# Attention with a token-routed feed-forward: the MoE of each batch as two streams, set into the attention loop by a table

## The chip, the cores and the metric

One core of a Trainium2 chip runs the kernel. The metric is device time in microseconds, taken around the whole program; the kernel before needs 296.96 us (median of three runs, 294.28 to 300.0). One more execution was recorded by the hardware profiler and took 294.19 us, of which 291.8 us lie between its first and its last instruction.

## The reference: what is computed

Two parts, one after the other. The attention (8 batches, 12 heads, 448 tokens, head size 64) has a squared ReLU in place of the softmax; its result `x` is the input of a mixture-of-depths layer (hidden size 768, inner size 1024), which passes only the 128 tokens with the highest gate score of each batch through two matrices and adds the result, weighted with a sigmoid of the score, to those tokens.

```python
scores = scale * q @ k.T                      # per batch and head, 448 x 448
x = (np.maximum(scores, 0.0) ** 2 / S) @ v    # heads side by side: 448 x 768
score = x @ w_gate                            # 448 values of a batch
top_idx = np.argpartition(-score, 128)[:128]
h = np.maximum(x[top_idx] @ w1, 0.0)
out = x.copy()
out[top_idx] += sigmoid(score[top_idx])[:, None] * (h @ w2)
```

## The kernel before: how the work is tiled and ordered

Inputs are loaded as bf16 by DMAs that POOL issues (`load`, lines 79 to 100), a batch at a time into one of three buffers; `load(b + 2)` is issued at the start of batch `b`. The loop runs over 48 iterations `t`, each one pair of heads (six to a batch). Its parts:

- `transposes(t)` (L160, L166): 16 matmuls against the identity put q and k of the pair, transposed, into one PSUM tile, which VectorE copies to `qkt` (L171).
- `scores(t, c)` (L181, L185): for the key chunks 0 to 2 two matmuls, one for each head, each on 64 rows of the TensorE array (contraction 64); chunk 3 is one matmul on all 128 rows (the two heads' last 64 keys each, in a zero-padded form). `s_ps` has two buffers.
- `relu_square(t, c)`: ScalarE applies the ReLU (L193), VectorE squares (L194).
- `attend(t, c)` (L205): two matmuls, each on 64 columns of the array, accumulate chunk `c` into `o_ps`; after the last chunk ScalarE scales it into `xT` (L211).

So TensorE works in three array modes: row halves (scores of chunks 0 to 2), column halves (transposes, attend) and the full array (chunk 3 and all of the MoE but a few small steps).

The MoE of a batch, `moe(b)` (lines 217 to 331), is one generator: gate scores (L222, then `bc`, L225), `x` transposed back in four chunks (`x_chunk`, L231, copied by VectorE, L234), the scores as columns (L240 and a chain of five small VectorE steps, L243 to L249), the rank of every token by comparing it with all others (`rank_chunk`, L256, four times), a one-hot matrix (`hot`, L272), the list of chosen tokens (`sel`, L279), the gathering matmuls (`xe`, L296), the two matrices (`h`, L307; `ye`, L320) and an indirect DMA that adds the result to the output (L327), behind a plain DMA of all of `x` (L268). All its PSUM tiles rotate through one pool of two buffers, `m_ps`. `advance` runs the generator from two places of each iteration, as far as the costs written into its `yield`s allow; the MoE of a batch is spread so over the six iterations of the next batch, and the last one follows the loop.

The order is written out by hand; each engine runs its instructions in that order, so an instruction that waits holds up all that follow it on its engine.

```python
for t in range(NT + 1):
    scores(t, 0); scores(t, 1); relu_square(t, 0); relu_square(t, 1)
    attend(t - 1, 2); attend(t - 1, 3)
    transposes(t + 1)
    advance(share)
    scores(t, 2); scores(t, 3); relu_square(t, 2); relu_square(t, 3)
    attend(t, 0); attend(t, 1)
    advance(share)
```

Of the kernel before, what the change touches and what calls it, by code (L numbers as in the profile page):

```python
# [20 lines left out]
def kernel(  # L21
# [27 lines left out]
    qt_pool = ctx.enter_context(tc.tile_pool(name="qt", bufs=3))  # L49
# [10 lines left out]
    m_ps_pool = ctx.enter_context(tc.tile_pool(name="m_ps", bufs=2, space=PSUM))  # L60
# [156 lines left out]
    def moe(b):  # L217
        xTb = xT.pop(b)
        x_sb = x_pool.tile([P, NC, HD], BF16, name="x_sb")
        sc_ps = m_ps_pool.tile([128, S], FP32, name="sc_ps", tag="m")  # L220
        for m in range(NM):
            nc.tensor.matmul(out=sc_ps, lhsT=wg_rep[:, m, :], rhs=xTb[:, m, :],  # L222
                             start=(m == 0), stop=(m == NM - 1))
        bc = small.tile([128, S], FP32, name="bc")
        nc.scalar.copy(out=bc, in_=sc_ps)  # L225
        yield 1.1

        def x_chunk(c):
            x_ps = m_ps_pool.tile([P, HD], BF16, name="x_ps", tag="m")
# [6 lines left out]
        x_chunk(0)  # L236
        yield 0.35
        col_ps = m_ps_pool.tile([P, NC], FP32, name="col_ps", tag="m")
        for c in range(NC):
            nc.tensor.matmul(out=col_ps[:, c:c + 1], lhsT=bc[0:1, c * P:(c + 1) * P],  # L240
                             rhs=one_f, is_transpose=True, start=(c == 0), stop=(c == NC - 1))
        cols = small.tile([P, NC], FP32, name="cols")
        nc.vector.tensor_copy(out=cols, in_=col_ps)  # L243
        tk = tok[b % 2]
        rem = small.tile([P, NC], FP32, name="rem")
        nc.vector.tensor_copy(out=tk[:, :, 2], in_=cols)
        nc.vector.tensor_tensor(out=rem, in0=cols, in1=tk[:, :, 2], op=ALU.subtract)
        nc.vector.tensor_copy(out=tk[:, :, 3], in_=rem)
        nc.vector.tensor_tensor(out=tk[:, :, 4], in0=rem, in1=tk[:, :, 3], op=ALU.subtract)  # L249
        yield 0.3  # L250

        rank = small.tile([P, NC], FP32, name="rank")
        trash = small.tile([P, S], BF16, name="trash")

        def rank_chunk(c):
# [19 lines left out]
        yield 0.6

        sel_ps = m_ps_pool.tile([CAP, 5], FP32, name="sel_ps", tag="m")
        for c in range(NC):
            nc.tensor.matmul(out=sel_ps, lhsT=hot[:, c, :], rhs=tk[:, c, :],  # L279
                             start=(c == 0), stop=(c == NC - 1))  # L280
        sel = small.tile([CAP, 5], FP32, name="sel")
        nc.vector.tensor_copy(out=sel, in_=sel_ps)
        idx = small.tile([CAP, 1], INT32, name="idx")
        nc.vector.tensor_tensor(out=idx, in0=sel[:, 0:1], in1=sel[:, 1:2], op=ALU.add)
        g = small.tile([CAP, 1], FP32, name="g")
        nc.vector.scalar_tensor_tensor(out=g, in0=sel[:, 4:5], scalar=sel[:, 3:4],
                                       in1=sel[:, 2:3], op0=ALU.add, op1=ALU.add)
        yield 0.2

        xeT = moe_pool.tile([128, NM, CAP], BF16, name="xeT")  # L290
        for half in range(2):
            ps = m_ps_pool.tile([128, 3, CAP], FP32, name="xe_ps", tag="m")
            for mm in range(3):
                m = half * 3 + mm
                for c in range(NC):
                    nc.tensor.matmul(out=ps[:, mm, :], lhsT=x_sb[:, c, m * 128:(m + 1) * 128],  # L296
                                     rhs=hot[:, c, :], start=(c == 0), stop=(c == NC - 1))
            nc.scalar.copy(out=xeT[:, half * 3:half * 3 + 3, :], in_=ps)  # L298
            yield 0.67

        hT = moe_pool.tile([128, NF, CAP], BF16, name="hT")
        for half in range(2):
            ps = m_ps_pool.tile([128, 4, CAP], FP32, name="h_ps", tag="m")
            for ff in range(4):
                f = half * 4 + ff
                for m in range(NM):
                    nc.tensor.matmul(out=ps[:, ff, :], lhsT=w1_sb[:, m, f * 128:(f + 1) * 128],  # L307
                                     rhs=xeT[:, m, :], start=(m == 0), stop=(m == NM - 1))
                if ff == 1:
                    yield 0.67  # L310
            nc.scalar.activation(out=hT[:, half * 4:half * 4 + 4, :], in_=ps, func=AF.Relu)
            yield 0.67

        nc.scalar.activation(out=g, in_=g, func=AF.Sigmoid)
        gye = moe_pool.tile([CAP, HD], FP32, name="gye")
        for half in range(2):
            cols_d = slice(half * 384, half * 384 + 384)
            ps = m_ps_pool.tile([CAP, 384], FP32, name="ye_ps", tag="m")
            for f in range(NF):
                nc.tensor.matmul(out=ps, lhsT=hT[:, f, :], rhs=w2_sb[:, f, cols_d],  # L320
                                 start=(f == 0), stop=(f == NF - 1))
                if f == 3:
                    yield 0.66
            nc.scalar.activation(out=gye[:, cols_d], in_=ps, func=AF.Copy, scale=g[:, 0:1])  # L324
            if half == 0:
                yield 0.66
        nc.gpsimd.indirect_dma_start(  # L327
            out=out.rearrange("b s d -> (b s) d"),
            out_offset=bass.IndirectOffsetOnAxis(ap=idx[:, :1], axis=0),
            in_=gye, in_offset=None, element_offset=b * S * HD, compute_op=ALU.add)  # L330
        yield 0.66


    MOE_US = 9.7
    active = []
    credit = [0.0]

    def advance(us):
        if not active:
            credit[0] = 0.0  # L340
            return
        credit[0] += us
        while active and credit[0] > 0.0:
            try:
                credit[0] -= next(active[0])
            except StopIteration:
                active.pop(0)

    tc_manual = tc.manual_schedule()
    with tc_manual:  # L350
        transposes(0)
        share = MOE_US / (2 * NHP) * 1.05
        for t in range(NT + 1):
            b, hp = divmod(t, NHP)
            if t < NT:
                scores(t, 0)
                scores(t, 1)
                relu_square(t, 0)
                relu_square(t, 1)
            if t > 0:  # L360
                attend(t - 1, 2)
                attend(t - 1, 3)
                if t % NHP == 0:
                    active.append(moe(t // NHP - 1))
            if t < NT:
                if hp == 0 and b + 2 < B:
                    load(b + 2, 0, H)
                if t + 1 < NT:
                    transposes(t + 1)
                advance(share)  # L370
                scores(t, 2)
                scores(t, 3)
                relu_square(t, 2)
                relu_square(t, 3)
                attend(t, 0)
                attend(t, 1)
                advance(share)
        while active:
            advance(10.0)
# [35 lines left out]
```

## Time and profile before

| | |
|---|---|
| median of three runs | 296.96 us (294.28 to 300.0) |
| profiled execution | 294.19 us, span 291.8 us |
| PE (TensorE matmul) busy | 231.8 us, 79% of the span |
| ACT (ScalarE) busy | 196.8 us, 67% |
| DVE (VectorE) busy | 184.4 us, 63% |
| POOL (GpSimd) busy | 88.8 us, 30% |
| mean granted TensorE clock | 0.918 of full speed |
| data moved | 34.20 MB |

Busy time is the union of the intervals in which an engine has an instruction running. A matmul's end is modelled and matmuls overlap, so what a matmul costs is read from start to start, not from its duration. The shares are means over stages with different limits: a head that waits for loads, six batches of like work, and a tail after the last head pair.

### The profile page before, as it was taken

The page shows a single profiled execution, that of the slowest core. Times are in us where ns is not written, and L with a number is a line of the kernel's source. Part 1 is how long each engine was busy: PE and PEld are TensorE (multiplying, and loading weights), DVE is VectorE, ACT ScalarE, POOL GpSimd, SP SyncE. Part 2 cuts the span into 40 slices and gives each one's busy share as a digit, 9 for nine tenths or more (in the row PEclk, how much of TensorE's full clock was granted, in tenths as well). Part 3 has the DMA queues.
Part 4 walks back from the last instruction along what each step waited for, and adds up shares of the span by engine and source line. Part 5 has one row for each costly group of instructions (what it writes and reads, how often), then busy time and mean ns, then how long its engine had stood idle before and what let it go on. Part 6 is the DMA issues. An engine that isn't in the chain of part 4 may idle for free.

```text
span 291.8 us, 6198 instructions
## 1 busy us (share of the span) xinstructions
PE 231.8 (79%) x2496; PEld 132.2 (45%) x2496; DVE 184.4 (63%) x426; ACT 196.8 (67%) x306; POOL 88.8 (30%) x128
## 2 busy tenths in 40 slices
PE   1598924799959997899978998699869995997570
PEld 1144413355436644465445644464436542644550
DVE  4268742955696658835696658956796669755400
ACT  1389940589846987458875996689759995794130
POOL 8989206771181027100541018100200020002010
PEclk9999995699998999579986999999999999999595
DMA  3999999999599709950399009950322030403504
GB/s 42 104 144 125 211 208 173 170 196 194 198 127 180 223 0 142 201 189 2 40 173 286 31 0 138 202 191 2 55 80 113 0 56 1 191 0 49 195 0 54
DMA packets 41723, 34.20 MB, mean 117 GB/s; under 512 B 14944, under 2 KB 39008, under 8 KB 40800
## 3 DMA queue, kind: packets, MB, share of 16 engines
q0 software_dynamic: 41696, 33.83, 69.6%
q8 instruction: 19, 0.31, 0.4%
q14 instruction: 8, 0.07, 0.1%
HBM read 39.32 MB, written 14.16 MB: 183 GB/s over the span
## 4 chain that ended last, share of the span: by engine, by line
PE 46%; DVE 19%; DMA 10%; ACT 9%; POOL 8%; issue 5%; POOLq 1%; ACTq 0%
PE o_ps L205 10%; PE s_ps L181 9%; PE h_ps L307 7%; ACT r_sb L193 7%; DMA k_sb<-in_k_dram 7%; PE ye_ps L320 7%; DVE trash L256 5%; DVE a_sb L194 4%; PE xe_ps L296 4%; DVE x_sb L234 4%; PE s_ps L185 3%; DMA q_sb<-in_q_dram 2%; PE t_ps L166 2%; DMA out_dram<-x_sb 2%; POOL k_sb L89 2%
## 5 line engine op out<-in xcount | busy, mean ns | idle before, releaser
L193 ACT ACTIVATE r_sb<-s_ps 128x896 bf16<-128x896 f32 x192 | 148.2, 829 | 48.4 <-PE s_ps L181 47.6
L194 DVE TENSOR_TENSOR a_sb<-r_sb 128x896 bf16<-128x896 bf16 x192 | 103.4, 564 | 69.2 <-ACT r_sb L193 68.5
L205 PE MATMUL o_ps<-a_sb,v_sb 128*64 128x448 bf16 x384 | 59.5, 384 | 3.0 <-DVE a_sb L194 2.6
L327 POOL DMA_INDIRECT out_dram<-gye,idx x8 | 13.1, 1638 | 127.1 <-ACT gye L324 117.9
L181 PE MATMUL s_ps<-qkt 64*128 64x448 bf16 x288 | 49.2, 376 | 2.7 <-ACT r_sb L193 1.3
L171 DVE COPY qkt<-t_ps 128x960 bf16<-128x960 bf16 x48 | 31.2, 651 | 14.1 <-PE t_ps L166 14.1
L205 PEld LDWEIGHTS <-v_sb 128*64 128x64 bf16 x384 | 19.2, 110 | 33.0 <-issue 27.5
L160 PE MATMUL t_ps<-ident,q_sb 112*64 112x112 bf16 x384 | 19.6, 225 | 15.5 <-DMA q_sb<-in_q_dram 10.1
L307 PE MATMUL h_ps<-xeT,w_sb 128*128 128x128 bf16 x384 | 28.0, 227 | 1.3 <-ACT xeT L298 1.3
L160 PEld LDWEIGHTS <-q_sb 112*64 112x64 bf16 x384 | 17.8, 118 | 21.4 <-DMA q_sb<-in_q_dram 15.8
L92 POOL DMA_DIRECT2D v_sb<-in_v_dram x22 | 17.5, 796 | 31.8 <-DMA q_sb<-in_q_dram 12.5
L231 PE MATMUL x_ps<-ident,xT_sb 128*112 128x128 bf16 x192 | 16.7, 231 | 12.6 <-DVE x_sb L234 10.6
L211 ACT ACTIVATE xT_sb<-o_ps 128x448 bf16<-128x448 f32 x48 | 26.6, 554 | 0.1
L307 PEld LDWEIGHTS <-w_sb 128*128 128x128 bf16 x384 | 23.3, 102 | 5.3 <-issue 4.0
L181 PEld LDWEIGHTS <-qkt 64*128 64x128 bf16 x288 | 12.6, 94 | 27.9 <-issue 19.5
L320 PE MATMUL ye_ps<-w_sb,hT 128*128 128x384 bf16 x128 | 25.0, 328 | 0.0
L298 ACT CAST xeT<-xe_ps 128x384 bf16<-128x384 f32 x16 | 7.6, 478 | 25.0 <-PE xe_ps L296 24.3
L166 PE MATMUL t_ps<-ident,k_sb 128*64 128x128 bf16 x384 | 21.9, 232 | 2.7 <-DMA k_sb<-in_k_dram 2.6
L89 POOL DMA_DIRECT2D v_sb<-in_v_dram x22 | 20.1, 921 | 8.6 <-DMA w_sb<-in_moe_w_dram 7.2
L231 PEld LDWEIGHTS <-xT_sb 128*112 128x112 bf16 x192 | 13.8, 137 | 17.6 <-issue 17.1
L256 DVE SCALAR_TENSOR_TENSOR trash<-bc,cols,tie 112x448 bf16<-112x448 f32 x32 | 21.7, 677 | 0.0
L89 POOL DMA_DIRECT2D k_sb<-in_k_dram x22 | 20.9, 954 | 0.0
(54 smaller groups left out, 217.6 us busy)
## 6 DMA issues: line engine op xcount, KB each, us to landing
out_dram<-x_sb POOLq DMA_DIRECT2D x8, 1344.0 KB, 8.8
q_sb<-in_q_dram POOLq DMA_DIRECT2D x6, 672.0 KB, 9.8
w_sb<-in_moe_w_dram POOLq DMA_DIRECT2D x2, 1536.0 KB, 14.4
k_sb<-in_k_dram POOLq DMA_DIRECT2D x12, 192.0 KB, 10.0
v_sb<-in_v_dram POOLq DMA_DIRECT2D x12, 192.0 KB, 6.9
k_sb<-in_k_dram POOLq DMA_DIRECT2D x12, 144.0 KB, 9.9
v_sb<-in_v_dram POOLq DMA_DIRECT2D x12, 144.0 KB, 10.8
q_sb<-in_q_dram POOLq DMA_DIRECT2D x2, 224.0 KB, 4.3
```

The costliest lines, as they stand in the source:

```text
L89: nc.gpsimd.dma_start(out=t[0:64, hs, 0:lo, :], in_=src[b, hs, 0:64 * lo].rearrange("h (p c) d -> p h c d", c=lo))
L160: nc.tensor.matmul(out=ps[64 * hh:64 * hh + 64, c * P:(c + 1) * P], lhsT=qs[:, h0 + hh, c, :], rhs=ident[:P, :P], is_transpose=True, start ...
L166: nc.tensor.matmul(out=ps[64 * hh:64 * hh + 64, S + c * 128:S + (c + 1) * 128], lhsT=ks[:, h0 + hh, c, :], rhs=ident, is_transpose=True, s ...
L171: nc.vector.tensor_copy(out=sb, in_=ps)
L181: nc.tensor.matmul(out=ps[:, hh, :S], lhsT=sb[rows, S + c * 128:S + (c + 1) * 128], rhs=sb[rows, :S], start=True, stop=True)
L193: nc.scalar.activation(out=r[:, :n], in_=ps[:, :n, :S], func=AF.Relu)
L194: nc.vector.tensor_tensor(out=a[:, :n], in0=r[:, :n], in1=r[:, :n], op=ALU.mult)
L205: nc.tensor.matmul(out=o_ps[t][rows, :], lhsT=vs[:, 2 * hp + hh, c, :], rhs=a[:, hh if c < 3 else 0, :], start=(c == 0), stop=(c == 3), sk ...
L231: nc.tensor.matmul(out=x_ps[:, m * 128:(m + 1) * 128], lhsT=xTb[:, m, c * P:(c + 1) * P], rhs=ident, is_transpose=True, start=(m == 0), st ...
L256: nc.vector.scalar_tensor_tensor(out=trash, in0=bc[:P, :], scalar=cols[:, c:c + 1], in1=tie[:, c, :], op0=ALU.subtract, op1=ALU.is_ge, acc ...
L307: nc.tensor.matmul(out=ps[:, ff, :], lhsT=w1_sb[:, m, f * 128:(f + 1) * 128], rhs=xeT[:, m, :], start=(m == 0), stop=(m == NM - 1))
L320: nc.tensor.matmul(out=ps, lhsT=hT[:, f, :], rhs=w2_sb[:, f, cols_d], start=(f == 0), stop=(f == NF - 1))
```

## The change

The attention loop is reordered: the transposes run two iterations ahead (with four `qkt` buffers), all of `attend(t - 1)` stands together behind the first two scores of `t`, in the chunk order 0, 1, 3, 2, and the second half of an iteration computes chunk 3 before chunk 2. The MoE is split in two sets of steps. `moe_rank(b)` (gate to gathering) runs during batch `b + 1`, `moe_ffn(b)` (the two matrices) during batch `b + 2`; two tables say which steps stand in which of the twelve half iterations. The pool `m_ps` of two buffers becomes two pools of one buffer each: `ma_ps` (gate, columns, `x`, `sel`, first half of `xe`) and `mb_ps` (second half of `xe`, `h`, `ye`). What each step computes is as before.

```diff
...
-    qt_pool = ctx.enter_context(tc.tile_pool(name="qt", bufs=3))
+    qt_pool = ctx.enter_context(tc.tile_pool(name="qt", bufs=4))
...
-    m_ps_pool = ctx.enter_context(tc.tile_pool(name="m_ps", bufs=2, space=PSUM))
+    ma_ps_pool = ctx.enter_context(tc.tile_pool(name="ma_ps", bufs=1, space=PSUM))
+    mb_ps_pool = ctx.enter_context(tc.tile_pool(name="mb_ps", bufs=1, space=PSUM))
...
-                             stop=(c == 3), skip_group_check=True)
-        if c == 3:
+                             stop=(c == 2), skip_group_check=True)
+        if c == 2:
...
-    def moe(b):
+    def moe_rank(b):
...
+        def gate(m0, m1):
+            if m0 == 0:
+                ps["sc"] = ma_ps_pool.tile([128, S], FP32, name="sc_ps", tag="m")
+            for m in range(m0, m1):
+                nc.tensor.matmul(out=ps["sc"], lhsT=wg_rep[:, m, :], rhs=xTb[:, m, :],
+                                 start=(m == 0), stop=(m == NM - 1))
+            if m1 == NM:
+                nc.scalar.copy(out=bc, in_=ps["sc"])
...
+        def gather(half):
+            xe = (ma_ps_pool, mb_ps_pool)[half].tile([128, 3, CAP], FP32, name="xe_ps", tag="m")
...
+    def moe_ffn(b, idx, g, xeT):
...
+        def hidden(f):
+            if f % 4 == 0:
+                ps["h"] = mb_ps_pool.tile([128, 4, CAP], FP32, name="h_ps", tag="m")
+            for m in range(NM):
+                nc.tensor.matmul(out=ps["h"][:, f % 4, :],
+                                 lhsT=w1_sb[:, m, f * 128:(f + 1) * 128],
+                                 rhs=xeT[:, m, :], start=(m == 0), stop=(m == NM - 1))
+            if f % 4 == 3:
+                nc.scalar.activation(out=hT[:, f - 3:f + 1, :], in_=ps["h"], func=AF.Relu)
...
+        def project(half, f0, f1):
...
+    RANK = {
+        1: [("gate", 0, 6)], 2: [("col",)], 3: [("x", 0)], 4: [("x", 1), ("rank", 0)],
+        5: [("rank", 1)], 6: [("x", 2)], 7: [("rank", 2)], 8: [("x", 3), ("rank", 3)],
+        9: [("hot",)], 10: [("sel",)], 11: [("xe", 0), ("xe", 1)],
+    }
+    FFN = {
+        0: [("h", 0)], 1: [("h", 1)], 3: [("h", 2), ("h", 3)],
+        5: [("h", 4), ("h", 5), ("h", 6), ("h", 7)], 7: [("y", 0, 0, 8)], 9: [("y", 1, 0, 8)],
+    }
...
+    def moe(b, hs):
+
+        if b >= 1:
+            if hs == 1:
+                rank_steps[b - 1], handed[b - 1] = moe_rank(b - 1)
+            if hs >= 1:
+                place(RANK, rank_steps[b - 1], hs)
+        if b >= 2:
+            if hs == 0:
+                ffn_steps[b - 2] = moe_ffn(b - 2, *handed.pop(b - 2))
+            place(FFN, ffn_steps[b - 2], hs)
+
+    with tc.manual_schedule():
         transposes(0)
...
+        transposes(1)
+        for t in range(NT):
             b, hp = divmod(t, NHP)
...
+            scores(t, 0)
+            scores(t, 1)
+            relu_square(t, 0)
+            relu_square(t, 1)
             if t > 0:
...
+                for c in (0, 1, 3, 2):
+                    attend(t - 1, c)
+            if hp == 0 and b + 2 < B:
+                load(b + 2, 0, H)
+            if t + 2 < NT:
+                transposes(t + 2)
+            moe(b, 2 * hp)
+            scores(t, 3)
+            relu_square(t, 3)
+            scores(t, 2)
+            relu_square(t, 2)
+            moe(b, 2 * hp + 1)
+        for c in (0, 1, 3, 2):
+            attend(NT - 1, c)
+        for hs in range(12):
+            moe(B, hs)
+        ffn_steps[B - 1] = moe_ffn(B - 1, *handed.pop(B - 1))
+        for hs in range(12):
+            place(FFN, ffn_steps[B - 1], hs)
```

## Rows read from the trace of the kernel before

**Rows 1.** Windows: stretch, length, busy us of each engine, TensorE clock, DMA share, GB/s.

```profile
27.07:30.50 3.43, 2.95 (x34) 1.45 (x31) 2.74 (x5) 3.41 (x6) 3.43 (x7) 1.00 1.03 150
...
74.97:106.90 31.93, 27.95 (x315) 15.94 (x314) 22.93 (x52) 24.05 (x38) 8.64 (x11) 0.95 0.77 140
106.90:140.64 33.74, 30.49 (x313) 17.56 (x313) 22.45 (x52) 24.24 (x38) 8.54 (x11) 0.85 0.68 116
...
172.69:203.36 30.67, 26.84 (x315) 15.28 (x314) 22.32 (x52) 24.22 (x38) 8.53 (x11) 1.00 0.75 127
...
264.96:291.80 26.84, 12.69 (x128) 10.07 (x126) 6.36 (x21) 4.56 (x10) 3.76 (x3) 0.74 0.35 81
```

**Rows 2.** Waits of PE, 75 to 265 us: sum, times, longest (us).

```profile
PE x_ps L231 <- DVE x_sb L234: 7.7, 6, 3.2
PE sel_ps L279 <- DVE hot L272: 7.5, 5, 2.4
```

**Rows 3.** Timeline of PE, one iteration and a little more: start, us, instructions.

```profile
223.68 1.51 PE L307 MATMUL h_ps<-xeT,w_sb 128*128 128x128 bf16 x24
225.13 0.55 PE L181 MATMUL s_ps<-qkt 64*128 64x448 bf16 x4
225.61 0.57 PE L205 MATMUL o_ps<-a_sb,v_sb 128*64 128x448 bf16 x4
226.01 0.37 PE L160 MATMUL t_ps<-ident,q_sb 112*64 112x112 bf16 x8
...
226.53 0.84 PE L307 MATMUL h_ps<-xeT,w_sb 128*128 128x128 bf16 x12
227.31 0.36 PE L181 MATMUL s_ps<-qkt 64*128 64x448 bf16 x2
227.61 0.36 PE L185 MATMUL s_ps<-qkt 128*128 128x448 bf16 x1
227.90 0.57 PE L205 MATMUL o_ps<-a_sb,v_sb 128*64 128x448 bf16 x4
228.40 0.82 PE L320 MATMUL ye_ps<-w_sb,hT 128*128 128x384 bf16 x4
229.16 0.69 PE L181 MATMUL s_ps<-qkt 64*128 64x448 bf16 x4
```

**Rows 4.** Timeline of DVE, 241 to 245 us.

```profile
241.33 0.65 DVE L171 COPY qkt<-t_ps 128x960 bf16<-128x960 bf16 x1
241.90 0.15 DVE L243 COPY cols<-col_ps 112x4 f32<-112x4 f32 x1
...
242.78 0.68 DVE L256 SCALAR_TENSOR_TENSOR trash<-bc,cols,tie 112x448 bf16<-112x448 f32 x1
...
243.39 0.55 DVE L234 COPY x_sb<-x_ps 112x768 bf16<-112x768 bf16 x1
243.86 0.92 DVE L194 TENSOR_TENSOR a_sb<-r_sb 128x896 bf16<-128x896 bf16 x2
```

**Rows 5.** Timeline of ACT, first two ReLUs of that iteration (225.13 in Rows 3).

```profile
225.53 1.73 ACT L193 ACTIVATE r_sb<-s_ps 128x896 bf16<-128x896 f32 x2 [0.37 <-PE s_ps L181]
```

**Rows 6.** Timeline of PE: transposes of t = 8 and of t = 12.

```profile
48.92 0.61 PE L166 MATMUL t_ps<-ident,k_sb 128*64 128x128 bf16 x7 [0.93 <-DMA k_sb<-in_k_dram]
...
71.82 0.39 PE L160 MATMUL t_ps<-ident,q_sb 112*64 112x112 bf16 x8
```

**Rows 7.** Timeline of POOL: the last k load of batch 2 is issued.

```profile
52.88 0.69 POOL L92 DMA_DIRECT2D k_sb<-in_k_dram  x1
```

**Rows 8.** The page's DMA issues: KB each, median us to landing.

```profile
k_sb<-in_k_dram POOLq DMA_DIRECT2D x12, 192.0 KB, 10.0
```

**Rows 9.** Timeline of the tail, PE and ACT.

```profile
272.89 0.27 PE L279 MATMUL sel_ps<-tok,hot 112*128 112x5 bf16 x4 [2.98 <-DVE hot L272]
...
273.02 2.72 PE L296 MATMUL xe_ps<-hot,x_sb 112*128 112x128 bf16 x24
...
282.57 0.58 ACT L324 ACTIVATE gye<-ye_ps,g 128x384 f32<-128x384 f32 x1 [0.67 <-PE ye_ps L320]
```

More of the change, by code (lines that the diff above doesn't have):

```diff
@@ L212, in attend, with columns @@
                                  scale=o_scale)
-    def moe(b):
+    def moe_rank(b):
         xTb = xT.pop(b)
         x_sb = x_pool.tile([P, NC, HD], BF16, name="x_sb")
[L220 to L223, printed above, removed]
         bc = small.tile([128, S], FP32, name="bc")
-        nc.scalar.copy(out=bc, in_=sc_ps)
-        yield 1.1
+        cols = small.tile([P, NC], FP32, name="cols")
+        rem = small.tile([P, NC], FP32, name="rem")
+        rank = small.tile([P, NC], FP32, name="rank")
+        trash = small.tile([P, S], BF16, name="trash")
+        hot = small.tile([P, NC, CAP], BF16, name="hot")
+        sel = small.tile([CAP, 5], FP32, name="sel")
+        idx = small.tile([CAP, 1], INT32, name="idx")
+        g = small.tile([CAP, 1], FP32, name="g")
+        xeT = moe_pool.tile([128, NM, CAP], BF16, name="xeT")
+        tk = tok[b % 2]
+        ps = {}
+        def gate(m0, m1):
[6 more added lines that the diff above has]
+                nc.scalar.copy(out=bc, in_=ps["sc"])
+        def columns():
+            col_ps = ma_ps_pool.tile([P, NC], FP32, name="col_ps", tag="m")
+            for c in range(NC):
+                nc.tensor.matmul(out=col_ps[:, c:c + 1], lhsT=bc[0:1, c * P:(c + 1) * P],
+                                 rhs=one_f, is_transpose=True, start=(c == 0),
+                                 stop=(c == NC - 1))
+            nc.vector.tensor_copy(out=cols, in_=col_ps)
+            nc.vector.tensor_copy(out=tk[:, :, 2], in_=cols)
+            nc.vector.tensor_tensor(out=rem, in0=cols, in1=tk[:, :, 2], op=ALU.subtract)
+            nc.vector.tensor_copy(out=tk[:, :, 3], in_=rem)
+            nc.vector.tensor_tensor(out=tk[:, :, 4], in0=rem, in1=tk[:, :, 3], op=ALU.subtract)
@@ L228, in x_chunk @@
         def x_chunk(c):
[L229 removed]
+            x_ps = ma_ps_pool.tile([P, HD], BF16, name="x_ps", tag="m")
             for m in range(NM):
@@ L234, in x_chunk @@
             nc.vector.tensor_copy(out=x_sb[:, c, :], in_=x_ps)
[L236 to L253, printed above, removed]
+            if c == NC - 1:
+                nc.gpsimd.dma_start(out=out[b].rearrange("(p c) d -> p c d", c=NC), in_=x_sb)
         def rank_chunk(c):
@@ L275, in moe @@
[L275 to L292, printed above, removed]
+        def one_hot():
+            nc.vector.tensor_tensor(
+                out=hot, in0=slot_row.unsqueeze(1).to_broadcast([P, NC, CAP]),
+                in1=rank.unsqueeze(2).to_broadcast([P, NC, CAP]), op=ALU.is_equal)
@@ new lines, in select @@
+        def select():
+            sel_ps = ma_ps_pool.tile([CAP, 5], FP32, name="sel_ps", tag="m")
+            for c in range(NC):
+                nc.tensor.matmul(out=sel_ps, lhsT=hot[:, c, :], rhs=tk[:, c, :],
+                                 start=(c == 0), stop=(c == NC - 1))
+            nc.vector.tensor_copy(out=sel, in_=sel_ps)
+            nc.vector.tensor_tensor(out=idx, in0=sel[:, 0:1], in1=sel[:, 1:2], op=ALU.add)
+            nc.vector.scalar_tensor_tensor(out=g, in0=sel[:, 4:5], scalar=sel[:, 3:4],
+                                           in1=sel[:, 2:3], op0=ALU.add, op1=ALU.add)
@@ L295, in moe @@
                 for c in range(NC):
-                    nc.tensor.matmul(out=ps[:, mm, :], lhsT=x_sb[:, c, m * 128:(m + 1) * 128],
+                    nc.tensor.matmul(out=xe[:, mm, :], lhsT=x_sb[:, c, m * 128:(m + 1) * 128],
                                      rhs=hot[:, c, :], start=(c == 0), stop=(c == NC - 1))
-            nc.scalar.copy(out=xeT[:, half * 3:half * 3 + 3, :], in_=ps)
-            yield 0.67
-        hT = moe_pool.tile([128, NF, CAP], BF16, name="hT")
[L302 to L312, printed above, removed]
@@ L327, in moe @@
[L327 to L347, printed above, removed]
@@ L349 @@
-    tc_manual = tc.manual_schedule()
-    with tc_manual:
+            nc.scalar.copy(out=xeT[:, half * 3:half * 3 + 3, :], in_=xe)
+        steps = {
+            "gate": gate, "col": columns, "x": x_chunk, "rank": rank_chunk,
+            "hot": one_hot, "sel": select, "xe": gather,
+        }
+        return steps, (idx, g, xeT)
+    def moe_ffn(b, idx, g, xeT):
+        hT = moe_pool.tile([128, NF, CAP], BF16, name="hT")
+        gye = moe_pool.tile([CAP, HD], FP32, name="gye")
+        ps = {}
+        def hidden(f):
[8 more added lines that the diff above has]
+        def project(half, f0, f1):
+            cols_d = slice(half * 384, half * 384 + 384)
+            if f0 == 0:
+                ps["y"] = mb_ps_pool.tile([CAP, 384], FP32, name="ye_ps", tag="m")
+                if half == 0:
+                    nc.scalar.activation(out=g, in_=g, func=AF.Sigmoid)
+            for f in range(f0, f1):
+                nc.tensor.matmul(out=ps["y"], lhsT=hT[:, f, :], rhs=w2_sb[:, f, cols_d],
+                                 start=(f == 0), stop=(f == NF - 1))
+            if f1 == NF:
+                nc.scalar.activation(out=gye[:, cols_d], in_=ps["y"], func=AF.Copy,
+                                     scale=g[:, 0:1])
+                if half == 1:
+                    nc.gpsimd.indirect_dma_start(
+                        out=out.rearrange("b s d -> (b s) d"),
+                        out_offset=bass.IndirectOffsetOnAxis(ap=idx[:, :1], axis=0),
+                        in_=gye, in_offset=None, element_offset=b * S * HD,
+                        compute_op=ALU.add)
+        return {"h": hidden, "y": project}
@@ new lines, with place @@
+    RANK = {
[6 more added lines that the diff above has]
+        5: [("h", 4), ("h", 5), ("h", 6), ("h", 7)], 7: [("y", 0, 0, 8)], 9: [("y", 1, 0, 8)],
+    }
+    rank_steps, ffn_steps, handed = {}, {}, {}
+    def place(table, steps, hs):
+        for name, *args in table.get(hs, ()):
+            steps[name](*args)
@@ L354 @@
             b, hp = divmod(t, NHP)
[L355 to L359, printed above, removed]
-            if t > 0:
[L361 to L377, printed above, removed]
```

29 lines of the change are left out of this document (removed).

## The prediction, made before the change was run

> **What bounds the kernel now.** I read the windows first, cut where the scores of t = 12, 18, 24 and so on begin, so that each holds one batch of attention with the MoE of the batch before. A batch takes 30.67 us at full clock and 33.74 us in a window with a granted clock of 0.85 [rows 1]; the six from 74.97 to 264.96 average 31.7 us. In none does an engine reach its span: at full clock PE is busy 26.84 us, ACT 24.22, DVE 22.32. Attention alone (the window at 27 us, no MoE yet) is bound by ACT: 3.41 of 3.43 us busy [rows 1]. With the MoE, PE carries most, yet it idles 30.67 - 26.84 = 3.83 us a batch.
>
> The waits of PE say where: from 75 to 265 us it stood 7.7 us before `x_ps` until VectorE had copied the chunk before, and 7.5 us before `sel_ps` until `hot` was there, up to 3.2 us at once [rows 2]. That is 15.2 of the idle, 2.5 us a batch: the ranking is a chain PE, DVE, PE, DVE, emitted almost without work between its links, and TensorE, which runs its instructions in order, stops with the attention behind it.
>
> The timeline of PE shows the second cost. 24 `h` matmuls take 225.13 - 223.68 = 1.45 us with what follows, 12 take 0.78: 0.67 us for 12, 0.056 each, and 0.11 left over once, at the change from the full array to row halves [rows 3]. Four attend matmuls take 0.40 us before the transposes (same mode) and 0.50 before full-array work: again 0.10 [rows 3]. So a change of array mode costs about 0.10 us.
>
> **The change, part by part.** All times start to start.
>
> *Array modes.* Before, an iteration goes rows (scores 0, 1), columns (attend, transposes), full (MoE), rows (scores 2), full (scores 3), columns (attend), full (MoE), back to rows: seven changes. After: rows, columns (all of attend, transposes), full (MoE, then scores 3), rows (scores 2), full (MoE), rows: five. 2 x 0.10 x 6 = 1.2 us a batch saved.
>
> *The ranking spread by table.* The 3.83 us of idle go, if no link stands directly before the next. One PE stream needs 26.84 us, of which some 0.4 is waiting hidden inside groups (four score matmuls take 0.48 us unhindered, 0.62 where the next group comes late; two such iterations a batch by the same view). 26.84 - 0.4 - 1.2 = 25.2 us of PE work.
>
> *What waits next.* I laid one iteration out on three queues, its first score at 0. ACT starts the ReLU 0.40 us after its score is issued and takes 0.81 us for one, 0.93 to the end (two: 1.73) [rows 5]. PE: attend 0.48 to 1.3, transposes to 1.75, a MoE step, scores 3 at about 2.1, scores 2 at 2.4, the odd MoE step from 2.7, next iteration near 4.15. The ReLUs of chunks 0 and 1 end at 1.33 and 2.14, so scores 3 and 2 find their buffers free; ACT has 24.2 us of work a batch [rows 1] and keeps up. DVE does two squares (0.53 each), then the `qkt` copy, 0.57, done at about 3.3, and only then the MoE step [rows 4]. Two hand-overs fail there, because the new pools have one buffer: `x` chunk 0 (half step 3) waits until DVE has copied the columns, 3.5 against 2.7: 0.8 us; `xe` (step 11) waits for the `sel` copy in the same way, 0.85 us. The other steps have a half iteration more. In the iterations with two ranks DVE needs 1.9 for the four squares + 0.57 + 0.47 + 2 x 0.61 = 4.2 us, against PE's 4.15: the last attend waits some 0.1, twice. Together 1.9 us: **25.2 + 1.9 = 27.1 us a batch**. Bounds of this unknown: no wait at all, 25.2; twice the waits, 29.0.
>
> *The head.* The loads of batch 1 bind it: the k transposes of t = 8 get their data at 48.92 us, 0.6 us from done [rows 6]. DMAs come in the same order, so this moment stays. But these transposes now stand in iteration 6, not 7: one iteration more is left behind the wait. From 49.5: the rest of iteration 6 with the gate, at half clock as after PE's wait in the tail [rows 1, 9], 3.4 us; iteration 7, part of it at half clock, 5.1; 8 and 10, bound by DVE, 4.2 each; 9, 3.6; 11 with its wait, 4.8. Batch 2 starts at 74.8, against 74.97 before, although this batch now carries no FFN. Starting with `transposes(1)` delays the first scores by some 5 us, which the wait for t = 8 absorbs; without that cover it would cost them. The transposes of t = 12, at 71.82 before [rows 6], come at about 66; their last k load is issued at 52.88 [rows 7], lands about 10 us later [rows 8], so it is there by 63: cost nothing, up to 3 if it lands late. POOL's order changes little: the scatter of a batch now stands behind the next loads, not before them.
>
> *The tail.* The FFN of batch 6 leaves the loop and runs beside the ranking of batch 7, then comes the FFN of 7. Before, gate to `sel` is 272.89 - 264.96 = 7.9 us, a chain on DVE [rows 1, 9]. After, x chunk 2 stands behind four `h` steps (24 x 0.056 = 1.3 us) and x chunk 3 behind eight `ye` matmuls (1.3 us; four take 0.76 with a mode change [rows 3]), the start behind `h` 0: 10.65 by the same lay-out, 2.7 more. Given back: the gathering takes 2.72 us for 24 matmuls, as the clock had fallen during the wait of 2.98 [rows 9]; at 0.056 it takes 1.5, and PE is now kept busy: 1.2 less. 26.84 + 2.7 - 1.2 = 28.3 us. Bounds: 26 (all hidden in the DVE chain) and 31 (all of the FFN's PE work added, 48 x 0.056 + 16 x 0.16 = 5.3 us).
>
> *The sum.* 74.8 + 6 x 27.1 + 0.8 (last attend) + 28.3 = 266.5 us of span; with the 2.4 us around the span 268.9, against 294.19. The median of the runs stands 0.9% above the profiled execution, so I forecast **271 us**.
>
> **The rivals.** Each is 106.3 (all but the loop) + 6 x the batch.
>
> 1. *Nothing waits*: 25.2 us, 258 us. ACT's 24.2 allow it. Against: the two hand-overs have a reason in the code.
>
> 2. *The clock*: the long idle goes, but short waits remain in almost every iteration, and PE falls back to half clock as in the window at 0.85, 3.1 us longer than the one at full clock [rows 1]. Batch 30.2, 287.5 us. Against: the window at full clock has 3.83 us of idle too. The Trainium skill (TensorE: Matmul & The Clock Gate, "A second HAM failure mode: psum-queue depth-cycling") describes this case, short idles between groups of matmuls at each turn of the PSUM buffers that make the clock oscillate. The full-clock row here speaks against it.
>
> 3. *The change does not do what it says*: what PE no longer loses to the ranking it loses to the chain score, ReLU, square, attend, now that attend needs all four squares at once. The batch stays at 30.7: 290.5 us. For: the last square ends just before its attend in my lay-out. Against: ACT and DVE have 6 and 8 us to spare.
>
> 4. *Slower*: the single buffers. Twelve tiles a batch pass through the two pools, each standing in PE's order until the one before is read; ACT and DVE read them only after the attention work queued ahead. I found 0.8 us for two; if all twelve cost it, the batch is 25.2 + 9.6 = 34.8, 315 us. It decides from 0.63 us each (32.75 a batch). For: `x_ps` waited up to 3.2 us even with two buffers [rows 2]. Against: most tiles have 2 us or more between them in the table. The Trainium skill (Perfetto Trace Analysis, "Optimization Strategy") reads a gap that repeats as too few PSUM buffers; by that rule cutting a rotation of two to single buffers is the wrong way.
>
> **The numbers.** Chances: forecast 0.70, rival 1 0.05, rival 2 0.09, rival 3 0.08, rival 4 0.08. About 2% is what a measurement of this kernel can tell: the limits are 291.0 and 302.9. Forecast, rival 1 and most of rival 2 are faster: 0.82. Rival 3 and the rest of 2: within 2%, 0.10. Rival 4: slower, 0.08. The range reaches from rival 1 to rivals 2 and 3, which takes in the bounds of the waits (258 to 280 by the sum) and of the tail: 257 to 291.
>
> **What would show it.** PE: idle per batch near 2 us, no wait of `sel_ps` on `hot` above 1 us, waits of `x_ps` on `cols` and `xe_ps` on `sel` of about 0.8 once a batch. Full clock from 60 us to the last attend. Transposes of t = 8 at 48.9; batch 2 starting near 75, the last attend near 238, gate to `sel` in the tail near 10.7. Wrong if a batch stays above 30 us, if waits on `a_sb` or `r_sb` take the place of those on `hot`, or if the loads of batch 2 hold t = 12.

## The result and the profile after

The changed kernel takes 268.98 us (median of four runs, 268.7 to 270.86) against 297.18 (294.28 to 300.0) in the same sessions: a ratio of 0.909, 95% interval 0.901 to 0.918. Ratios, here and below, leave out runs over 1.5% above the fastest run of the same kernel. The profiled execution took 268.7 us with a span of 266.6; 271 was forecast, with a span of 266.5.

The windows of the changed kernel, cut where the scores of t = 12, 18, 24 and so on begin, one before them and the tail last, with some left out. Columns as in [rows 1].

```profile
50.00:74.48 24.48, 20.57 (x219) 10.91 (x219) 21.03 (x53) 19.85 (x29) 15.79 (x24) 0.89 1.39 199
74.48:102.37 27.89, 25.25 (x314) 15.39 (x313) 21.68 (x51) 25.42 (x39) 3.18 (x5) 1.00 0.77 150
...
182.63:209.37 26.74, 24.98 (x314) 15.34 (x314) 21.68 (x51) 23.98 (x38) 2.25 (x2) 1.00 0.25 68
209.37:235.45 26.08, 24.15 (x282) 14.35 (x280) 20.70 (x49) 23.96 (x38) 2.17 (x2) 1.00 0.25 69
236.33:266.60 30.27, 16.78 (x192) 12.48 (x190) 6.63 (x21) 6.93 (x14) 5.30 (x4) 0.89 0.40 85
```

Against [rows 1] a batch at full clock falls from 30.67 to 26.74 us; PE has 24.98 us busy in place of 26.84 and idles 1.76 in place of 3.83. ACT's and DVE's work is about as before. The granted clock is 1.00 in every batch, where [rows 1] have 0.95 and 0.85 in their first two; the third stood at 0.89:

```profile
140.64:172.69 32.05, 28.80 (x313) 16.42 (x314) 22.45 (x52) 24.42 (x38) 8.54 (x11) 0.89 0.71 121
```

These three batches took 1.3, 3.1 and 1.4 us more than the 30.67 at full clock. So some 5.8 us of what the loop gained is the lower clock that no longer comes, and the rest is shorter batches. Of the 25.2 us of span, the head gave 0.5 (t = 12 begins at 74.48, before at 74.97), the loop 28.1 (from there to the start of the last batch's gate or, after, its first FFN step: 189.99 us before, 236.33 - 74.48 = 161.85 after), and the tail took 3.4 back: 30.27 against 26.84.

The waits of PE from 75 to 236 us, to be read against [rows 2]:

```profile
PE xe_ps L290 <- DVE sel L280: 4.4, 6, 0.8
PE x_ps L258 <- DVE cols L249: 4.4, 6, 0.8
PE s_ps L182 <- ACT r_sb L194: 1.2, 3, 0.5
PE s_ps L186 <- ACT r_sb L194: 0.4, 1, 0.4
PE o_ps L206 <- DVE a_sb L195: 0.3, 2, 0.2
```

No line is left of `sel_ps` on `hot` or of `x_ps` on `x_sb`; the two that stand at the top are the ones that the single buffers were forecast to make, once a batch each. Two iterations of PE's timeline, against [rows 3]:

```profile
189.31 0.36 PE L182 MATMUL s_ps<-qkt 64*128 64x448 bf16 x2
190.40 0.49 PE L258 MATMUL x_ps<-ident,xT_sb 128*112 128x128 bf16 x6 [0.73 <-DVE cols L249]
190.73 0.83 PE L309 MATMUL h_ps<-xeT,w_sb 128*128 128x128 bf16 x12
191.50 0.55 PE L182 MATMUL s_ps<-qkt 64*128 64x448 bf16 x4
191.98 0.95 PE L206 MATMUL o_ps<-a_sb,v_sb 128*64 128x448 bf16 x8
192.76 0.36 PE L161 MATMUL t_ps<-ident,q_sb 112*64 112x112 bf16 x8
...
193.28 0.54 PE L258 MATMUL x_ps<-ident,xT_sb 128*112 128x128 bf16 x6
193.66 0.35 PE L186 MATMUL s_ps<-qkt 128*128 128x448 bf16 x1
193.94 0.36 PE L182 MATMUL s_ps<-qkt 64*128 64x448 bf16 x2
194.24 1.51 PE L309 MATMUL h_ps<-xeT,w_sb 128*128 128x128 bf16 x24
195.68 0.55 PE L182 MATMUL s_ps<-qkt 64*128 64x448 bf16 x4
196.16 1.21 PE L206 MATMUL o_ps<-a_sb,v_sb 128*64 128x448 bf16 x8
197.19 0.39 PE L161 MATMUL t_ps<-ident,q_sb 112*64 112x112 bf16 x8
```

Eight attend matmuls take 0.78 us (191.98 to 192.76), and 1.03 (196.16 to 197.19) where the last square comes late after two ranks: a hidden wait of 0.25. Scores 3 follow the `x` chunk in the same array mode: six transposes take 0.38 us there (193.28 to 193.66), 0.06 each, while an `x` chunk with row-half scores behind it needs 0.48 (202.37 to 202.85 in the kernel with the table alone, below).

### The profile page after: what moved, and what is told of

It reads as the page before. It is cut to its first block, busy times and chain, and to the rows that moved or that the text cites. A ratio compares the mean times of both kernels' runs of the same rounds, so it can differ in the third digit from the quotient of the medians.

```text
span 266.6 us, 6187 instructions
## 1 busy us (share of the span) xinstructions
PE 211.8 (79%) x2496; PEld 126.8 (48%) x2496; DVE 179.8 (67%) x426; ACT 196.1 (74%) x306; POOL 88.2 (33%) x128
## 4 chain that ended last, share of the span: by engine, by line
DVE 33%; PE 25%; ACT 14%; DMA 11%; POOL 8%; issue 5%; POOLq 1%; ACTq 0%
DVE a_sb L195 15%; ACT r_sb L194 12%; DMA k_sb<-in_k_dram 7%; DVE qkt L172 7%; DVE trash L266 5%; PE xe_ps L290 5%; PE h_ps L309 4%; PE s_ps L182 4%; DVE x_sb L261 4%; PE sc_ps L238 4%; PE o_ps L206 3%; DMA out_dram<-gye,idx 2%; DMA q_sb<-in_q_dram 2%; POOL k_sb L90 2%; POOL k_sb L93 2%
## 5 line engine op out<-in xcount | busy, mean ns | idle before, releaser
L182 PE MATMUL s_ps<-qkt 64*128 64x448 bf16 x288 | 47.2, 368 | 7.7 <-ACT r_sb L194 7.5
L206 PE MATMUL o_ps<-a_sb,v_sb 128*64 128x448 bf16 x384 | 49.7, 369 | 1.3 <-DVE a_sb L195 0.3
L263 POOL DMA_DIRECT2D out_dram<-x_sb x8 | 4.5, 564 | 86.5 <-DVE x_sb L261 84.6
L309 PE MATMUL h_ps<-xeT,w_sb 128*128 128x128 bf16 x384 | 26.5, 219 | 1.3 <-ACT hT L313 0.7
L182 PEld LDWEIGHTS <-qkt 64*128 64x128 bf16 x288 | 11.4, 94 | 32.1 <-issue 29.5
L93 POOL DMA_DIRECT2D v_sb<-in_v_dram x22 | 16.8, 766 | 29.4 <-DMA q_sb<-in_q_dram 20.7
L322 PE MATMUL ye_ps<-w_sb,hT 128*128 128x384 bf16 x128 | 23.5, 327 | 2.1 <-ACT gye L325 1.1
L90 POOL DMA_DIRECT2D v_sb<-in_v_dram x22 | 18.7, 848 | 11.0 <-DMA w_sb<-in_moe_w_dram 7.3
L313 ACT ACTIVATE hT<-h_ps 128x512 bf16<-128x512 f32 x16 | 9.6, 597 | 13.4 <-PE h_ps L309 13.4
L93 POOL DMA_DIRECT2D k_sb<-in_k_dram x22 | 19.0, 865 | 0.4 <-issue 0.4
```

The source lines that it names most:

```text
L90: nc.gpsimd.dma_start(out=t[0:64, hs, 0:lo, :], in_=src[b, hs, 0:64 * lo].rearrange("h (p c) d -> p h c d", c=lo))
L93: nc.gpsimd.dma_start(out=t[64:128, hs, 0:hi, :], in_=src[b, hs, 64 * lo:S].rearrange("h (p c) d -> p h c d", c=hi))
L182: nc.tensor.matmul(out=ps[:, hh, :S], lhsT=sb[rows, S + c * 128:S + (c + 1) * 128], rhs=sb[rows, :S], start=True, stop=True)
L309: nc.tensor.matmul(out=ps["h"][:, f % 4, :], lhsT=w1_sb[:, m, f * 128:(f + 1) * 128], rhs=xeT[:, m, :], start=(m == 0), stop=(m == NM - 1))
L322: nc.tensor.matmul(out=ps["y"], lhsT=hT[:, f, :], rhs=w2_sb[:, f, cols_d], start=(f == 0), stop=(f == NF - 1))
```

## The experiments

Each kernel ran beside the kernel before in three rounds; ratios are to it.

**The two halves of the change alone.** The first kernel has the new attention order and the MoE of before:

```diff
 (kernel before, loop)
...
+                for c in (0, 1, 3, 2):
+                    attend(t - 1, c)
                 if t % NHP == 0:
                     active.append(moe(t // NHP - 1))
...
+            if t + 2 < NT:
+                transposes(t + 2)
+            advance(share)
+            scores(t, 3)
+            relu_square(t, 3)
+            scores(t, 2)
+            relu_square(t, 2)
+            advance(share)
...
```

> The new order of the attention and the transposes two ahead, with the MoE of before (one generator, pool of two buffers, spread by its written costs). My theory: only the two array-mode changes go (1.2 us a batch); the ranking chain still stops PE. Batch 29.5 to 30.5 us (the upper end if the clock still dips), batch 2 starts at about 78 us, tail 26.8 as before: 285 to 291 us in all. Rival (the regrouped attention is the main gain, the streams matter little): 268 to 276 us.

Measured: 299.86 us, ratio 1.018 (1.009 to 1.026). Slower than both theories allow. Two windows of this kernel, columns as in [rows 1]:

```profile
179.00:212.10 33.10, 29.28 (x342) 17.33 (x340) 23.85 (x54) 26.11 (x42) 9.41 (x12) 0.95 0.69 118
212.10:242.40 30.30, 25.90 (x317) 15.62 (x314) 22.67 (x52) 24.03 (x39) 2.29 (x3) 1.00 0.21 59
```

Only the second window is at full clock; there the gates of successive batches are 30.24 us apart, against 30.64 before. The waits of PE from 75 to 236 us in this kernel:

```profile
PE x_ps L231 <- DVE x_sb L234: 8.4, 5, 2.5
PE s_ps L181 <- ACT r_sb L193: 5.6, 14, 0.7
PE sel_ps L279 <- DVE hot L272: 3.6, 4, 1.6
```

So two mode changes fewer took about 0.9 us from PE's busy time in a batch (25.90 against 26.84), near the 1.2 that they were put at, but its idle time grew from 3.8 to 4.4, and 0.4 of the batch is left as gain. A wait of scores on the ReLU, which [rows 2] do not have, stands beside the ranking's own. In the batch at full clock it comes twice, where only one `x` chunk or four `ye` matmuls stand between scores 2 and the next scores; that the ReLU is late there because PE has too little other work is read from the order, and no run separates it.

What makes this kernel slower is its head. Its t = 12 begins at 83.57 us, before at 74.97: 8.6 us later, while loop and tail together take 2.7 less (span 297.7 against 291.8). Transposes two ahead leave one iteration more behind the wait for t = 8 (4.1 us in a run below), and the whole ranking of batch 0 moved behind it too (gate at 49.71 us, at 34.48 before). The table has its gate there as well (50.40), but spreads the ranking and leaves the FFN to the next batch.

The second has the streams by table with attend split as before and scores 2 before 3:

```diff
 (changed kernel, loop)
-                for c in (0, 1, 3, 2):
-                    attend(t - 1, c)
+                attend(t - 1, 2)
+                attend(t - 1, 3)
...
+            scores(t, 2)
             scores(t, 3)
+            relu_square(t, 2)
             relu_square(t, 3)
-            scores(t, 2)
-            relu_square(t, 2)
+            attend(t, 0)
+            attend(t, 1)
...
```

> The MoE streams by table and everything else of the changed kernel, but attend split again (chunks 2, 3 behind the first scores, 0, 1 behind the second) and scores 2 before 3: seven array-mode changes an iteration in place of five. My theory: 0.2 us an iteration more on PE in the 42 iterations after the loads, 8.4 us: 277 us, batch 28.0, and the granted clock stays full. Rival (grouping is the main gain): 286 us or more. Rival (a mode change is free where other waits cover it): 269 to 271.

Measured: 281.79 us, ratio 0.956 (0.948 to 0.965), full clock from 80 us, batch 28.82 (gates at 194.82 and 223.64). Between my 277 and the rival's 286. The table alone gives half of the 28 us, and it keeps the clock up, which the order alone does not. At full clock a batch takes 30.64 us before, 30.24 with the order alone, 28.82 with the table alone and 26.74 with both: the order is worth 0.4 us without the table and 2.1 with it. What within the table does it (the spread ranking, the FFN a batch later, the two pools) no run separates. The timeline of PE in this kernel shows why a split attend costs more than its mode changes:

```profile
197.80 0.37 PE L246 MATMUL col_ps<-one_f,bc 1*112 1x1 f32 x4
198.10 0.36 PE L182 MATMUL s_ps<-qkt 64*128 64x448 bf16 x2
198.57 0.35 PE L186 MATMUL s_ps<-qkt 128*128 128x448 bf16 x1
199.01 0.60 PE L206 MATMUL o_ps<-a_sb,v_sb 128*64 128x448 bf16 x4
199.87 0.49 PE L258 MATMUL x_ps<-ident,xT_sb 128*112 128x128 bf16 x6 [0.25 <-DVE cols L249]
```

and among its waits from 75 to 236 us the longest in total is

```profile
PE s_ps L186 <- ACT r_sb L194: 2.6, 10, 0.4
```

Scores 2 and 3 take 0.47 and 0.44 us here, 0.30 and 0.29 in [rows 3]: with four attend matmuls fewer ahead of them PE is at these scores before the ReLU has emptied their buffer, 0.3 us an iteration, 1.9 a batch. Two mode changes make 1.2, and the waits at `cols` and `sel` are 1.0 shorter (0.25 and 0.26): 26.74 + 1.9 + 1.2 - 1.0 = 28.8, a rough sum, since the late squares, some 0.5 us a batch in the changed kernel, hardly show here. So all of attend stands between the two halves of the scores not only for the array's mode but as cover for the ReLU.

**The order of the chunks.** Scores 2 before 3, attend kept together:

```diff
 (changed kernel, loop)
-                for c in (0, 1, 3, 2):
+                for c in range(4):
...
+            scores(t, 2)
+            relu_square(t, 2)
             scores(t, 3)
             relu_square(t, 3)
-            scores(t, 2)
-            relu_square(t, 2)
...
```

> The changed kernel with scores 2 before scores 3 (and attend in the order 0 to 3). The array-mode changes stay at five an iteration. It tells apart why the split attend cost 2.1 us a batch and not the 1.2 of two mode changes: if by the order (the long chunk 2 now needs its buffer earlier and the short chunk 3 stands last, its scores waiting for the ReLU of chunk 1), the batch grows from 26.75 to 27.5 or more, 273 us; if by the split alone, the time stays within 1 us of 269.

Measured: 269.26 us, ratio 0.917 (0.909 to 0.926); gates at 185.94 and 212.69, a batch of 26.75. The order of the chunks is worth nothing; the split alone costs.

**The two waits at the single buffers.**

```diff
 (changed kernel, moe and RANK)
-                place(RANK, rank_steps[b - 1], hs)
         if b >= 2:
...
             place(FFN, ffn_steps[b - 2], hs)
+        if b >= 1 and hs >= 1:
+            place(RANK, rank_steps[b - 1], hs)
...
-        11: [("xe", 0), ("xe", 1)],
+        11: [("xe", 1), ("xe", 0)],
```

> The changed kernel with the FFN steps ahead of the ranking steps within a half iteration, and the second half of the gathering (the other pool) ahead of the first. In the trace of the changed kernel PE stands 0.73 us before x chunk 0 and 0.81 before the gathering, once a batch each. My theory (single buffer, read late by VectorE): 12 h matmuls of 0.67 us now cover the first and 12 gathering matmuls of 0.67 the second, 1.3 us a batch over 6.5 batches: 260 us, batch 25.4. Rival (PE is no longer what sets the pace, ScalarE with 24.0 of 26.7 us is): the wait moves to scores on the ReLU or attend on the square, 265 us or more.

Measured: 261.92 us, ratio 0.889 (0.880 to 0.897); gates at 181.04 and 206.50, a batch of 25.46 (25.66 on the mean of the four from 103.86 on), where 25.4 was expected. Neither wait is among those of PE any more, and nothing of size took their place (scores on the ReLU: 1.7 us in 160). PE is busy 25.73 of 26.00 us in a window of this kernel: it is what sets the pace, and the pools' single buffers cost only where the table puts a step directly behind the one whose tile still fills the buffer.

**The head.** Transposes one iteration ahead in place of two:

```diff
 (changed kernel, loop)
-        transposes(1)
...
-            if t + 2 < NT:
-                transposes(t + 2)
+            if t + 1 < NT:
+                transposes(t + 1)
```

> The changed kernel with the transposes one iteration ahead, as before, in place of two. My theory: the transposes of t = 8 wait for their data until 48.9 us either way, but one iteration less is left behind the wait: 3.4 to 4 us less, 265 us, batch 2 starting near 71; the qkt copy (done at 3.3 us of an iteration that takes 4.4) is still in time. Rival (the depth of two hides the copy, one ahead makes scores wait for qkt each time): loop batches 0.3 us or more an iteration longer, 270 us or more.

Measured: 263.97 us, ratio 0.895 (0.887 to 0.902): 5.0 us less, 4.1 by the spans. The k transposes of t = 8 still run at 49.36, the gate of the last batch stands at 232.54 us in place of 236.68, and the batches are as long as before (26.74). The iteration left behind the wait is what the depth of two costs, and the copy does not need it: from 75 us on PE never waits for `qkt`; before that it does, 3.5 us in all, of which all but 0.35 stands ahead of the load wait, which covers it.

The weights loaded behind batch 2:

```diff
 (changed kernel, set-up and loop)
-    nc.gpsimd.dma_start(out=w1_sb, ...)
-    nc.gpsimd.dma_start(out=w2_sb, ...)
     load(1, 4, H)
...
                 load(b + 2, 0, H)
+                if t == 0:
+                    nc.gpsimd.dma_start(out=w1_sb, ...)
+                    nc.gpsimd.dma_start(out=w2_sb, ...)
```

> The changed kernel with the loads of the two weight matrices issued behind the loads of batch 2, in place of ahead of the second part of batch 1. My theory (the head is bound by that order of the DMAs: the transposes of t = 8 stand until 48.9 us behind 3 MB of weights, some 15 us of transfer, which nobody needs before the FFN of batch 0 at about 76 us): the transposes of t = 8 find their data when they come (36 to 38 us), batch 2 starts at 62 to 66 us, 257 to 261 us in all. Rival (the sum of the transfers binds the head, whatever their order): the wait moves to t = 12 or to the first h matmuls, 265 us or more.

Measured: 255.09 us, ratio 0.868 (0.858 to 0.878): 13.9 us less, 12.8 by the spans. PE's timeline where the wait had been, against [rows 6]:

```profile
38.28 0.37 PE L159 MATMUL t_ps<-ident,q_sb 112*64 112x112 bf16 x8
38.48 0.39 PE L165 MATMUL t_ps<-ident,k_sb 128*64 128x128 bf16 x8
38.80 0.36 PE L184 MATMUL s_ps<-qkt 128*128 128x448 bf16 x1
39.10 0.36 PE L180 MATMUL s_ps<-qkt 64*128 64x448 bf16 x2
39.39 1.31 PE L236 MATMUL sc_ps<-xT_sb,wg_rep 128*128 128x448 bf16 x6
```

The transposes of t = 8 come at 38.28 and wait for nothing; the gate runs at full clock (1.31 us; 2.42 in the changed kernel, after the wait). Batch 2 begins at 61.76 and finds its loads and weights there. So the head was not bound by the sum of the transfers but by their order, and this, not the MoE, was the largest item left.

**The tail.** Both pools for the last FFN:

```diff
 (changed kernel, moe_ffn)
-                ps["h"] = mb_ps_pool.tile(
+                ps["h"] = (ma_ps_pool if b == B - 1 and f == 4 else mb_ps_pool).tile(
-                ps["y"] = mb_ps_pool.tile(
+                ps["y"] = (ma_ps_pool if b == B - 1 and half == 1 else mb_ps_pool).tile(
```

> The changed kernel, in which the FFN of the last batch alone takes its PSUM tiles in turn from both pools. In its tail PE stood 0.57 to 0.72 us four times, before h, h, ye and ye. My theory (the single buffer: a tile waits until ScalarE has read the one before; that is the term the forecast of the tail left out): three of the four go, 2.0 us less, 267 us. Rival (the end hangs on the chain through ScalarE and the scatter, not on PE): 268 to 269 us.

Measured: 268.43 us, ratio 0.914 (0.906 to 0.921): the rival's time. PE is faster as expected, the last `gye` begins at 255.05 us in place of 257.66, and the last scatter hardly moves. Three waits of PE in the last FFN of the changed kernel, and its last `gye`:

```profile
251.80 1.50 PE L309 MATMUL h_ps<-xeT,w_sb 128*128 128x128 bf16 x24 [0.69 <-ACT hT L313]
253.98 1.46 PE L322 MATMUL ye_ps<-w_sb,hT 128*128 128x384 bf16 x8 [0.69 <-ACT hT L313]
256.16 1.46 PE L322 MATMUL ye_ps<-w_sb,hT 128*128 128x384 bf16 x8 [0.72 <-ACT gye L325]
257.66 0.58 ACT L325 ACTIVATE gye<-ye_ps,g 128x384 f32<-128x384 f32 x1 [1.55 <-PE ye_ps L322]
```

POOL in the tail, first before the change, then in the changed kernel, then in this one:

```profile
265.33 1.60 POOL L327 DMA_INDIRECT out_dram<-gye,idx  x1 [17.53 <-ACT gye L324]
271.81 0.58 POOL L268 DMA_DIRECT2D out_dram<-x_sb  x1 [4.88 <-DVE x_sb L234]
283.61 1.59 POOL L327 DMA_INDIRECT out_dram<-gye,idx  x1 [11.23 <-ACT gye L324]
```

```profile
245.95 0.58 POOL L263 DMA_DIRECT2D out_dram<-x_sb  x1 [7.84 <-DVE x_sb L261]
251.78 1.58 POOL L328 DMA_INDIRECT out_dram<-gye,idx  x1 [5.26 <-ACT hT L313]
258.70 1.56 POOL L328 DMA_INDIRECT out_dram<-gye,idx  x1 [5.34 <-ACT gye L325]
```

```profile
245.69 0.57 POOL L263 DMA_DIRECT2D out_dram<-x_sb  x1 [7.78 <-DVE x_sb L261]
251.61 1.58 POOL L328 DMA_INDIRECT out_dram<-gye,idx  x1 [5.35 <-ACT hT L313]
258.49 1.56 POOL L328 DMA_INDIRECT out_dram<-gye,idx  x1 [5.30 <-issue]
```

The steps are the same to 0.1 us: 5.8 from the plain DMA of batch 7 to the scatter of batch 6, whose data had been ready since about 247.5, and 6.9 from there to the scatter of batch 7. `hT`, which the rows name for the scatter of batch 6, is no input of it and only happened to end near; in this kernel the last wait names no engine. In the first kernel under "All of it" the profile names the write itself:

```profile
234.71 1.56 POOL L326 DMA_INDIRECT out_dram<-gye,idx  x1 [4.99 <-DMA out_dram<-gye,idx]
```

All three writes go into one output tensor, and in these rows each waits until the one before has landed (from issue to landing a plain DMA takes 5.1 us in this tail, a scatter 5.6). Before the change the scatter of batch 6 was issued as the tail began, and the two writes behind it were released by their data.

In the changed kernel a second path ends at the same moment: its last `gye` ends at 257.66 + 0.58 = 258.24 us, 0.46 before the scatter that needs it, the same distance as before the change (282.57 + 0.58 [rows 9], 283.61). So PE with its waits and the chain of writes let the last scatter go at about the same time. With the waits of PE gone it goes at 258.49 in place of 258.70, and the plain DMA at the head of the chain was 0.26 earlier in that run anyway.

To move the head of that chain, the four `x` chunks of the last batch, and with them its plain DMA, come first in the tail, and these chunks and the last two FFNs take both pools (the pools' lines are left out here):

```diff
 (changed kernel, after the loop)
-        for hs in range(12):
-            moe(B, hs)
+        rs, handed[B - 1] = moe_rank(B - 1)
+        fs = moe_ffn(B - 2, *handed.pop(B - 2))
+        for steps, name, *args in (
+                (rs, "gate", 0, 6), (rs, "x", 0), (rs, "col"), (rs, "x", 1), (rs, "x", 2),
+                (rs, "x", 3), (rs, "rank", 0), (rs, "rank", 1), (rs, "rank", 2), (rs, "rank", 3),
+                (rs, "hot"), (fs, "h", 0), (fs, "h", 1), (fs, "h", 2), (fs, "h", 3),
+                (fs, "h", 4), (fs, "h", 5), (fs, "h", 6), (fs, "h", 7), (fs, "y", 0, 0, 8),
+                (rs, "sel"), (fs, "y", 1, 0, 8), (rs, "xe", 1), (rs, "xe", 0)):
+            steps[name](*args)
```

> The changed kernel with another order after the loop only: the four x chunks of the last batch come first, so that its plain output DMA is issued about 3.5 us earlier, and the FFN of the two last batches takes both pools in turn. With both pools alone the last gye was ready 2.6 us earlier and the end moved by 0.3 us. My theory (the three writes to the output at the end, plain DMA of batch 7, scatter of 6, scatter of 7, each wait for the one before to land, 5.3 us each, and that chain sets the end): 2.5 to 3.5 us less, 266 us. Rival (the chain of the last batch through PE, DVE and ACT sets the end): no more than the 0.5 of the pools, 268 us or more.

Measured: 267.36 us, ratio 0.915 (0.903 to 0.927), 1.6 less than the changed kernel, between the two theories by the total. In the profiled execution all of it came 1.6 us later from the first gate on (52.06 against 50.40); its tail is 265.8 - 237.93 = 27.9 us against 30.27, 2.4 shorter. POOL in this tail:

```profile
244.11 0.58 POOL L263 DMA_DIRECT2D out_dram<-x_sb  x1 [4.35 <-DVE trash L266]
250.89 1.58 POOL L328 DMA_INDIRECT out_dram<-gye,idx  x1 [6.20 <-ACT xeT L292]
257.87 1.56 POOL L328 DMA_INDIRECT out_dram<-gye,idx  x1 [5.40 <-ACT gye L325]
```

The plain DMA comes 6.2 us after the tail's start in place of 9.6, and the end comes only 2.4 earlier. For the last scatter the rows name `gye`, which ends at 257.40 us, 0.47 before it; that path became 2.4 us shorter too (19.5 us from the tail's start in place of 21.9), by the pools and the new order. The edit shortens both paths, so this run does not tell which of them sets the end.

**All of it.** The first run joins FFN steps first, transposes one ahead, weights late and the pools; the second has the new tail too.

> FFN steps first and the gathering's halves swapped, transposes one ahead, weights late, and the tail with both pools, all in the changed kernel. The four gains by their own runs and forecasts are 7.1, 5.0, 8 to 12 and 2.0 us; one ahead and weights late act on the same wait, so 5.0 is not to be had twice: 247 to 252 us. Rival (with the head gone the loop falls behind its loads and the wait returns at a later batch): 255 us or more.

> This tail with FFN steps first, the gathering's halves swapped, transposes one ahead and the weights late: 244.8 us measured without it, 242 us with it by my theory, 244 by the rival of the run beside it.

Measured: 244.84 us, ratio 0.834 (0.826 to 0.842), and 242.74 us, ratio 0.831 (0.822 to 0.840). Both beat the kernel before by a sixth and the changed kernel by 24 and 26 us. The second is where it was expected, the first is below its 247 to 252: by the spans the four single gains are 6.6, 4.1, 12.8 and 0.3 us, 23.8 in all, and this kernel's is 23.7, so none was lost. With the weights late alone the first scores come at 13.20 us, here at 7.38: the delay of a start with `transposes(1)` that the prediction names, and that the load wait had covered. The wait for loads did not come back at a later batch: in the first of the two PE waits 3.5 us in all for q and k, at the very start.

## Why the prediction was right

- **Where PE's time went.** Right, and the largest term: the idle at `hot` and `x_sb` is gone, and a batch is 26.74 us against 27.1. PE's work was put at 25.2 us and its waits at 1.9; it is busy 24.98 and idle 1.76. The late squares hide some 0.56 us of waiting in the busy time, so the work is nearer 24.4 and the waits 2.3; where the other 0.8 us of work went no run shows. The two hand-overs were put at 0.8 and 0.85 us and took 0.73 and 0.81; with them covered the batch is 25.46 to 25.8. The late square was put at 0.1 twice and took 0.25 and 0.31.
- **The price of a mode change**, 0.10 us, holds in the rows after. As a gain of its own it was worth less: with the order alone a batch at full clock lost 0.4 us, not 1.2. With the table the grouping is worth 2.1 us, more than the 1.2, because keeping attend together also covers the ReLU, which the prediction put at nothing.
- **The head.** Wait until 48.88 (48.92 before), batch 2 at 74.48 (74.8 forecast), one iteration more behind the wait: 4.1 us by its own run, against 3.4 in the sum. The loads of batch 2 did not hold t = 12: its transposes came at 67.01 us without a wait.
- **The tail** is the term that was mis-sized: 28.3 forecast, 30.27 measured. From the tail's start to `sel` it was right (10.70 against 10.65). Two things in the rest were put at nothing. PE stands 0.57 to 0.72 us four times in the last FFN, three of them at the single buffers. And the step "POOL's order changes little" failed: the scatter of batch 6 now stands in the tail, behind the plain DMA of batch 7, and the last scatter behind both. The chain alone gives this tail: with both pools PE is 2.6 us faster and the end 0.3. That the waits of PE alone would give it too is read from the last `gye`; no run shortened the chain by itself. With both paths shorter the tail takes 27.9.
- **The loop** was 1.6 us shorter than the sum (6 x 27.1 + 0.8 against 161.85) and paid for most of that; the agreement of the span to 0.1 us is luck, errors that cancel. The sum put the loop at full clock throughout, and so it holds the 5.8 us of the lower clock as a gain that no term names. Scaling up to the median of the runs before added 2 us too many: the runs of the changed kernel lie within 2 us and begin at the profiled one.
- **The rivals.** The clock stays at 1.00 from 60 us to the last attend with waits of 0.8 us in it, so rival 2 did not come. The rule of the Trainium skill beside it (TensorE: Matmul & The Clock Gate, "A second HAM failure mode: psum-queue depth-cycling") does not describe this loop: its short idles left the clock at 1.00. Rival 3's wait of scores on the ReLU is real, but it costs where attend is split or the table is missing (2.6 and 5.6 us from 75 to 236 us, 1.6 in the changed kernel). Rival 4 had the right mechanism at the two places already in the sum, and no others in the loop: ten of the twelve hand-overs cost nothing there that the trace shows. The rule of the Trainium skill beside it (Perfetto Trace Analysis, "Optimization Strategy": repeated gaps can mean too few buffers) is borne out: the gap repeats once a batch at each of the two. A better order closed it without a buffer.

## What to carry to other kernels

When engines run in program order, price a regrouping with what it exposes: here two halves of a change gave +2% and -4% alone and -9% together. Look where a total comes from before reading it: the +2% was lost in the head, and in the loop the order was worth 0.4 us a batch without the table and 2.1 with it. A deeper pipeline moves work across fixed points, so count what then stands behind the last load wait and in the last chain of writes. And a lone wait on DMA early in the profile deserves the question whose bytes are ahead of it: moving two weight loads was worth half as much as the whole restructuring.
